# The second block of w1's columns in two parts: one load of six chunks becomes loads of two and of four

## The chip, the cores and the metric

The kernel runs on one core of a Trainium2 chip. The metric is device time in microseconds (us) of one execution. Matrix products run on TensorE (PE; its weight loads are listed as PEld), elementwise work on VectorE (DVE) and ScalarE (ACT), a few masks on GpSimd (POOL); SyncE (SP) issues most of the DMA transfers, ScalarE a few.

## What is computed

Two blocks share one layer norm of a sequence of 2048 tokens of width 448, and the second gates the first:

```python
xn = _layernorm(x)                       # (1, 2048, 448)
# A: linear attention, 16 heads of 28
q, k, v = split(xn @ wqkv)               # wqkv 448 x 1344
phi = lambda t: jnp.where(t > 0, t + 1, jnp.exp(t)) + 1e-6
kv = einsum("bhsd,bhse->bhde", phi(k), v); z = phi(k).sum(over s)
s = (phi(q) @ kv / (phi(q) . z + 1e-6)) @ wo
# B: a dense block with a squared relu
h = xn @ w1 + b1                         # w1 448 x 1792
g = silu(relu(h)**2 @ w2 + b2)           # w2 1792 x 448
out = x + s * g
```

All arrays are bfloat16.

## The kernel before

**Tiles.** Tokens stand in 16 tiles of 128 and four groups of four tiles (512 tokens). The width of 448 is contracted in three chunks of 128 rows (the "main" part of a weight) and one of 64. Those last 64 rows are loaded twice, into partitions 0 to 63 and 64 to 127 (the two "rests" of a weight), so that two half-height matmuls can run side by side in the two halves of TensorE. The 1792 columns of w1 are 14 chunks of 128; the product of group g with chunk fi is called H*g*.*fi*. K*si* is the key product of token tile si, Q*g*.*m* a query product, G*si* the gate product with w2.

**The order of work.** Every step is added to a list as an operation with its engine, what it reads and writes, and an estimated duration (`Program.add`). `Program.schedule` (L76 to L246) plays this through once: TensorE and SyncE keep the written order, and ScalarE, VectorE and GpSimd take their steps by readiness and due time. The planner also hands out the eight PSUM banks, in the order in which it expects them free. A DMA with an entry in the table `landing` (L1272) is taken to land at that time. What comes out is one fixed list for every engine and a set of semaphore waits (`Program.emit`). On the chip an engine does its list strictly in order.

**The start.** SyncE issues the loads in the written order (L453 to L469): x tiles 0, 1 and 2 to 3; the key weights; w1's first block (chunks 0 to 3) with its two rests; b1; w1's second block (chunks 4 to 9) with its two rests; x tiles 4 to 7; w1's third block (chunks 10 to 13) with its two rests. Then `late_loads` adds the row of b2, the two halves of w2 and the query weights with their rests, and after these follow x tiles 8 to 11 and 12 to 15, the value weights and wo. All of SyncE's transfers go through one queue that feeds the core's 16 DMA engines.

`load_main` (L435) is one DMA of 384 rows (three chunks of 128), `load_rest` (L442) with `part` one DMA of 64 rows. A row of the transfer is as long as the block is wide, two bytes for each column. `cuts` (L451) holds the blocks' borders, and `hh` (L781) makes a product wait for the main part and both rests of the block that its chunk lies in (names "w10", "w11", "w12").

**TensorE's first microseconds.** TensorE warms up on dummies (L1221), transposes x tiles 0 to 3 (L602, L626), and works on K0, K1, H0.0 and H0.1 as their data come (L801, L816, L829, L845). From there on the written order is H0.2 to H0.13 (L1360): `pe_four` takes four chunks at a time as two pairs that alternate, in the order H0.2 with H0.3 (first part, 8 matmuls), H0.4 with H0.5 (8), H0.2 with H0.3 (rest, 6), H0.4 with H0.5 (6), then likewise H0.6 with H0.7 and H0.8 with H0.9, then H0.10 with H0.11 and H0.12 with H0.13. All of these matmuls stand at L786. After them come K2, K3, G0 to G3 (L729, L1092), and Q0.0, Q0.1 (L739).

**VectorE beside it.** A K product becomes its feature map in three steps: the exponential on ScalarE (L707), a minimum (L712) and a maximum (L719) on VectorE. The last of them reads the product's PSUM bank for the last time. By the planner, VectorE's list around 11 us is: the maximum of K0, the layer-norm statistics of tiles 4 and 5 (L495 twice, L496 twice; they read x tiles 4 to 7's load), then the minimum and the maximum of K1, then the normalisation of tiles 4 and 5 (L525). H0.8 and H0.9 take the banks of H0.1 and K1.

Of the kernel before, what the change touches and what calls it, by code (L numbers as in the profile page):

```python
# [9 lines left out]
P = 128  # L10
S, D, F = 2048, 448, 1792
# [35 lines left out]
class Program:  # L47
# [6 lines left out]
    def add(self, eng, emit, reads=(), writes=(), dur=0.2, alts=(), nbytes=0, mode=None, label="", slow=1.0):  # L54
        op = Op(eng, emit, reads, writes, dur, alts, nbytes, mode, label)
        op.slow, op.behind, op.at = slow, None, None
        for t in op.reads:
            op.raw.add(self.writer[t])
            self.readers.setdefault(t, []).append(op)
        for t in op.writes:  # L60
            w = self.writer.get(t)
            if w is not None and w is not op:
                op.deps.add(w)
            for r in self.readers.get(t, ()):
                if r is not op:
                    op.deps.add(r)
            self.writer[t] = op
            self.readers[t] = [r for r in self.readers.get(t, ()) if r is op]
        op.raw.discard(op)
        op.deps |= op.raw  # L70
        for d in op.deps:
            d.succ.append(op)
        self.ops.append(op)
        return op
# [233 lines left out]
def bass_recurrent_scan__linear_attn_block__dense_activation_squared_relu__prompt_kernel(  # L308
    nc, A_x, A_wqkv, A_wo, B_x, B_w1, B_b1, B_w2, B_b2, out
):  # L310
    with ExitStack() as es:
# [21 lines left out]
        w_1 = sb("w_1", [P, 4, F], bf)  # L333
        w_2 = sb("w_2", [P, NF, D], bf)
        w_o = sb("w_o", [P, 7, D], bf)
        b1r = sb("b1r", [NF, P], bf)
# [83 lines left out]
        def tiles(t, lo, hi):  # L420
            if hi <= 2:
                return t[0][P * lo : P * hi].rearrange("(p s) d -> p s d", s=1)
            base, n = (2, 2) if hi <= 4 else (lo // 4 * 4, 4)
            v = t[0][P * base : P * (base + n)].rearrange("(p s) d -> p s d", s=n)
            return v[:, lo - base : hi - base, :]

        def dma(eng, dst, src, writes, nbytes, reads=(), dur=0.45, slow=1.0):
            return add(
                eng, lambda e, _: e.dma_start(dst, src), reads, writes, dur, nbytes=nbytes, label="dma" + str(writes[0]), slow=slow
            )  # L430

        def load_x(lo, hi, eng="sp"):
            dma(eng, x_tok[:, lo:hi, :], tiles(A_x, lo, hi), [("x", i) for i in range(lo, hi)], (hi - lo) * P * D * 2)

        def load_main(eng, w, src, name, lo, hi, c0=0, c1=3, off=0):  # L435
            dma(
                eng, w[:, c0:c1, lo:hi],
                src[128 * c0 : 128 * c1, off + lo : off + hi].rearrange("(c p) j -> p c j", p=P),
                [(name, c) for c in range(c0, c1)], 128 * (c1 - c0) * (hi - lo) * 2,
            )  # L440

        def load_rest(eng, w, src, name, lo, hi, off=0, part=None):  # L442
            for i in (0, 1) if part is None else (part,):
                dma(
                    eng, w[64 * i : 64 * i + 64, 3, lo:hi], src[384:448, off + lo : off + hi], [(name, 3 + i)],
                    64 * (hi - lo) * 2, ["actw"] if eng == "act" else (), dur=0.58,
                )

        wn = lambda name: [(name, i) for i in range(5)]
        HA = 2  # L450
        cuts = (0, 4 * P, 10 * P, F)  # L451
        add("act", lambda e, _: e.preload_act_table_set("natural_log_exp_and_others"), [], ["actw"], 1.25, label="table").prio = -1e6
        load_x(0, 1, "sp")  # L453
        load_x(1, 2, "sp")
# [5 lines left out]
        load_rest("sp", w_1, B_w1, "w10", cuts[0], cuts[1], part=0)  # L460
        load_rest("sp", w_1, B_w1, "w10", cuts[0], cuts[1], part=1)
        dma("sp", b1r[:, :], B_b1.rearrange("(f p) -> f p", p=P), ["b1r"], F * 2)
        load_main("sp", w_1, B_w1, "w11", cuts[1], cuts[2])
        load_rest("sp", w_1, B_w1, "w11", cuts[1], cuts[2], part=0)
        load_rest("sp", w_1, B_w1, "w11", cuts[1], cuts[2], part=1)
        load_x(4, 8, "sp")
        load_main("sp", w_1, B_w1, "w12", cuts[2], cuts[3])
        load_rest("sp", w_1, B_w1, "w12", cuts[2], cuts[3], part=0)
        load_rest("sp", w_1, B_w1, "w12", cuts[2], cuts[3], part=1)  # L469
        late_constants()  # L470

        def late_loads():
# [789 lines left out]
        for first, order in (  # L1262
# [6 lines left out]
                byname[b].prio = first + 1 + i  # L1269
            if first < -26:  # L1270
                byname[names[0]].prio = first
        landing = {("x", 0): 2.92, ("x", 1): 3.9, ("x", 2): 4.65, ("wk", 0): 5.7, ("wk", 3): 5.7, ("wk", 4): 7.2, ("w10", 0): 6.97, ("w10", 3): 7.2, ("w10", 4): 7.4, ("b1r", None): 7.5, ("w11", 0): 9.1, ("w11", 3): 9.4, ("w11", 4): 9.8, ("x", 4): 11.3}  # L1272
        for (name, k), t in landing.items():
            byname["dma" + str((name, k) if k is not None else name)].at = t

# [134 lines left out]
```

## Time and profile before

| | |
|---|---|
| median of 3 runs | 143.88 us (143.44 to 144.38) |
| the profiled execution's own time | 143.17 us |
| its span, first to last instruction | 141.9 us |
| TensorE busy | 138.5 us, 98% |
| VectorE, ScalarE, GpSimd busy | 103.0, 79.1, 6.2 us |
| DMA | 12.91 MB, mean 91 GB/s over the span |
| DMA engines' busy share | 0.9 or more from 3.5 to 17.7 us |

Times in the profile count from the first instruction. A row of the timeline gives start, length, engine, line, operation, output tile <- input tiles, the number of instructions merged, and in brackets the idle time before it and what ended it. In the DMA lists a row is tile <- source, issuing queue, count, KB each, and the us from issue to landing; in this trace all tiles of w1 and w2 are called `w`, K's `pk`, PSUM banks `pb`. A row of the table by stretches gives the stretch, its length, each engine's busy time, TensorE's granted clock, the share of the DMA engines that was busy (a little over 1 when packets overlap) and GB/s.

### The profile page before, as it was taken

What the parts mean: (1) busy time and instruction counts of PE and PEld (TensorE: products, weight loads), DVE (VectorE), ACT (ScalarE), POOL (GpSimd) and SP (SyncE); (2) the same over time, 40 slices, a digit from 0 to 9 for tenths busy, and PEclk for the clock granted to TensorE, in tenths of its full rate; (3) what the DMA queues carried; (4) which work ended last, traced back from release to release, by engine and by line L of the source; (5) the groups of instructions that cost most, each with busy time, mean ns of one, the idle gap of its engine ahead of it and who ended that gap; (6) DMA issues with size and microseconds to landing.
All of it is one profiled execution on the core that took longest, in us unless ns stands there. A gap on an engine that the chain in (4) does not pass through costs nothing.

```text
span 141.9 us, 3234 instructions
## 1 busy us (share of the span) xinstructions
PE 138.5 (98%) x1299; PEld 70.8 (50%) x1299; DVE 103.0 (73%) x222; ACT 79.1 (56%) x146; POOL 6.2 (4%) x40
## 2 busy tenths in 40 slices
PE   7999999999999999999999999999999999999992
PEld 7754445454444544444444444445547455555472
DVE  2756999699689897789777799786035516874875
ACT  3687998140888627697962767697139530301412
POOL 7900000000000000000000000000000000000000
PEclk9999999999999999999999999999999999999999
DMA  4999994239933000332000000000698000223033
GB/s 84 323 303 303 353 275 84 38 48 270 211 48 51 14 0 0 46 51 46 9 5 0 0 0 5 0 0 19 170 194 157 6 0 25 94 80 102 32 97 97
DMA packets 23516, 12.91 MB, mean 91 GB/s; under 512 B 14290, under 2 KB 22734, under 8 KB 23502
## 3 DMA queue, kind: packets, MB, share of 16 engines
q1 hardware_dynamic: 21710, 11.35, 31.5%
q10 hardware_dynamic: 1792, 1.36, 4.4%
q8 instruction: 10, 0.16, 0.5%
q14 instruction: 4, 0.03, 0.1%
HBM read 9.23 MB, written 1.90 MB: 78 GB/s over the span
## 4 chain that ended last, share of the span: by engine, by line
PE 97%; DVE 1%; issue 0%
PE pb L786 29%; PE pb L1092 22%; PE pb L1184 7%; PE pb L887 7%; PE pb L729 7%; PE pb L739 6%; PE pb L1109 4%; PE pb L1221 3%; PE pb L1149 3%; PE pb L866 1%; PE pb L829 1%; DVE gbuf L1173 1%; PE pb L893 1%; PE pb L801 1%; PE pb L1036 1%; PE pb L602 1%
## 5 line engine op out<-in xcount | busy, mean ns | idle before, releaser
L786 PE MATMUL pb<-xT,w 64*128 64x512 bf16 x378 | 43.6, 376 | 0.0
L1092 PE MATMUL pb<-w,r 64*128 64x448 bf16 x336 | 34.6, 349 | 0.0
L764 ACT ACTIVATE r<-pb,b1f 128x512 bf16<-128x512 f32 x40 | 25.7, 685 | 14.4 <-PE pb L786 14.1
L786 PEld LDWEIGHTS pb<-xT,w 64*128 64x128 bf16 x378 | 18.2, 94 | 21.9 <-DVE pk L719 0.3
L1092 PEld LDWEIGHTS pb<-w,r 64*128 64x128 bf16 x336 | 16.2, 94 | 16.0 <-issue 0.4
L776 ACT ACTIVATE r<-r 128x1024 bf16<-128x1024 bf16 x15 | 15.7, 1062 | 0.3
L761 DVE TENSOR_SCALAR r<-pb,b1f 128x512 bf16<-128x512 f32 x16 | 11.7, 744 | 4.1 <-PE pb L786 4.0
L1204 DVE TENSOR_TENSOR gbuf<-pb,gbuf 128x448 bf16<-128x448 f32 x14 | 8.1, 617 | 6.7 <-PE pb L1184 6.7
L495 DVE BATCH_NORM_STATS2 st<-x_tok 128x6 f32<-128x448 bf16 x16 | 9.6, 615 | 3.5 <-DMA x_tok<-in_A_x_dram 3.4
L729 PE MATMUL pb<-w_k,xT 64*128 64x448 bf16 x98 | 11.5, 349 | 0.0
L739 PE MATMUL pb<-xT,w_q 64*128 64x512 bf16 x84 | 11.0, 376 | 0.0
L1132 ACT ACTIVATE gbuf<-gbuf 128x448 bf16<-128x448 bf16 x14 | 7.0, 570 | 7.0 <-DVE gbuf L1082 5.9
L1184 PE MATMUL pb<-w_k,pqT 64*128 64x448 bf16 x96 | 10.5, 349 | 0.0
L1082 DVE TENSOR_TENSOR gbuf<-pb,b2b 128x448 bf16<-128x448 f32 x14 | 8.0, 613 | 3.4 <-PE pb L1092 2.0
L1000 DVE TENSOR_TENSOR pqT<-pqT,xT 128x2048 bf16<-128x2048 bf16 x3 | 3.7, 1222 | 8.5 <-DMA xT<-scr 8.5
L719 DVE SCALAR_TENSOR_TENSOR pk<-pb,pk 128x448 bf16<-128x448 f32 x16 | 9.6, 619 | 0.2
L707 ACT ACTIVATE pk<-pb 128x448 bf16<-128x448 f32 x16 | 7.8, 543 | 3.2 <-PE pb L729 2.5
L887 PE MATMUL pb<-pk,xn 128*128 128x448 bf16 x48 | 9.6, 353 | 0.0
L707 ACT ACTIVATE pqT<-pb 128x512 bf16<-128x512 f32 x12 | 6.5, 597 | 4.4 <-PE pb L739 4.4
L775 DVE TENSOR_TENSOR r<-r 128x1024 bf16<-128x1024 bf16 x13 | 8.6, 685 | 0.1
L923 DVE TENSOR_TENSOR zacc<-zacc,pk 128x448 f32<-128x448 f32 x13 | 8.0, 617 | 0.1
L525 DVE TENSOR_SCALAR xn<-x_tok,mv,rstd 128x448 bf16<-128x448 bf16 x16 | 7.4, 496 | 0.6 <-ACT rstd L507 0.6
(100 smaller groups left out, 133.4 us busy)
## 6 DMA issues: line engine op xcount, KB each, us to landing
w<-in_B_w_dram SPq DMA_DIRECT2D x2, 784.0 KB, 9.2
out_dram<-gbuf SPq DMA_DIRECT2D x14, 112.0 KB, 1.7
x_tok<-in_A_x_dram SPq DMA_DIRECT2D x3, 448.0 KB, 5.5
xT<-gbuf SPq DMA_DIRECT2D x32, 32.0 KB, 2.0
w<-in_B_w_dram SPq DMA_DIRECT2D x2, 384.0 KB, 5.7
xT<-scr SPq DMA_DIRECT2D x6, 112.0 KB
w<-in_B_w_dram SPq DMA_DIRECT2D x1, 576.0 KB, 5.4
xT<-scr ACTq DMA_DIRECT2D x5, 112.0 KB
```

The costliest lines, as they stand in the source:

```text
L495: add("dve", lambda e, _: e.bn_stats(st6[:, si, :], x_tok[:, si, :]), [("x", si)], [("st", si)], 0.61, label=f"bn{si}").prio = hp(si, 0)
L707: "act", lambda e, _: e.activation(out=slot, in_=ps(buf)[0:rows, 0:n], func=AF.Exp), [buf, "actw"],
L719: lambda e, _: e.scalar_tensor_tensor(out=slot, in0=ps(buf)[0:rows, 0:n], scalar=1.0 + 1e-6, in1=slot, op0=ALU.add, op1=ALU.max),
L729: return e.matmul(ps(b)[:, 0:D], x_tile(rows, si, c), w_k[rows, c, :], start=start, stop=stop)
L739: return e.matmul(ps(b)[:, 0:512], w_q[rows, c, m * P : (m + 1) * P], x_group(rows, g, c), start=start, stop=stop,)
L761: return e.tensor_scalar(out=slot, in0=ps(b)[:, 0:512], scalar1=b1f[:, fi : fi + 1], scalar2=0.0, op0=ALU.add, op1=ALU.max)
L764: return e.activation(out=slot, in_=ps(b)[:, 0:512], func=AF.Relu, bias=b1f[:, fi : fi + 1])
L776: return e.activation(out=both, in_=both, func=AF.Square)
L786: return e.matmul(ps(b)[:, 0:512], w_1[rows, c, fi * P : (fi + 1) * P], x_group(rows, g, c), start=start, stop=stop,)
L887: last = e.matmul(ps(b)[:, 0:D], xn_cols(si, c * P, (c + 1) * P), pk[:, si, :], start=(si == 0), stop=(si == NT - 1),)
L1092: return e.matmul(ps(b)[:, 0:D], r_cols(rows, fi, si), w_2[rows, fi, :], start=start, stop=stop)
L1184: return e.matmul(ps(b)[:, 0:D], w, msb[rows, c, :], start=start, stop=stop)
```

## The change

The second block of w1's columns is cut in two: chunks 4 and 5, and chunks 6 to 9. Each part has its own main DMA and its own two rests, so that three DMAs (576 KB, 96 KB, 96 KB) become six (192, 32, 32 and 384, 64, 64 KB), issued in this order ahead of x tiles 4 to 7. The last block is now called "w13". H0.4 and H0.5 (and the same chunks of the later groups) read "w11", H0.6 to H0.9 read "w12". The table `landing` has entries for the two parts in place of the one; the entry of x tiles 4 to 7 stays 11.3. The lists of TensorE, ScalarE, VectorE and GpSimd are in the order of before; SyncE's has three more issues.

```diff
-        cuts = (0, 4 * P, 10 * P, F)
+        cuts = (0, 4 * P, 6 * P, 10 * P, F)
...
-        load_main("sp", w_1, B_w1, "w11", cuts[1], cuts[2])
-        load_rest("sp", w_1, B_w1, "w11", cuts[1], cuts[2], part=0)
-        load_rest("sp", w_1, B_w1, "w11", cuts[1], cuts[2], part=1)
-        load_x(4, 8, "sp")
-        load_main("sp", w_1, B_w1, "w12", cuts[2], cuts[3])
-        load_rest("sp", w_1, B_w1, "w12", cuts[2], cuts[3], part=0)
-        load_rest("sp", w_1, B_w1, "w12", cuts[2], cuts[3], part=1)
+        for i in (1, 2, 3):
+            name = f"w1{i}"
+            load_main("sp", w_1, B_w1, name, cuts[i], cuts[i + 1])
+            load_rest("sp", w_1, B_w1, name, cuts[i], cuts[i + 1], part=0)
+            load_rest("sp", w_1, B_w1, name, cuts[i], cuts[i + 1], part=1)
+            if i == 2:
+                load_x(4, 8, "sp")
...
-        landing = {..., ("w11", 0): 9.1, ("w11", 3): 9.4, ("w11", 4): 9.8, ("x", 4): 11.3}
+        landing = {
...
+            ("w10", 3): 7.2, ("w10", 4): 7.4, ("b1r", None): 7.5, ("w11", 0): 8.2, ("w11", 3): 8.4, ("w11", 4): 8.6,
+            ("w12", 0): 9.7, ("w12", 3): 9.9, ("w12", 4): 10.1, ("x", 4): 11.3,
+        }
```

More of the change, by code (lines that the diff above doesn't have):

```diff
@@ L1271, in bass_recurrent_scan__linear_attn_block__dense_activation_squared_relu__prompt_kernel @@
                 byname[names[0]].prio = first
-        landing = {("x", 0): 2.92, ("x", 1): 3.9, ("x", 2): 4.65, ("wk", 0): 5.7, ("wk", 3): 5.7, ("wk", 4): 7.2, ("w10", 0): 6.97, ("w10", 3): 7.2, ("w10", 4): 7.4, ("b1r", None): 7.5, ("w11", 0): 9.1, ("w11", 3): 9.4, ("w11", 4): 9.8, ("x", 4): 11.3}
+        landing = {
[3 rows of a table added]
+        }
         for (name, k), t in landing.items():
```

1 row of the table landing is left out of this document.

## The prediction

> **What bounds the kernel now.** I read the chain that ended last first, because the change touches only loads of the first 20 us.
>
> ```profile
> PE 97%; DVE 1%; issue 0%
> ...
> 10.51 0.32 PE pb L845 x2
> 10.83 9.06 PE pb L786 x84
> ```
>
> TensorE sets the end nearly everywhere. From 10.83 us it works through the first group's H products (twelve column chunks, two of head work before them): 84 matmuls in 9.06 us, 0.108 us each, or 0.216 us for the two half-height matmuls of one step. The later run of 92 takes 9.93 us, the same 0.108. So this stage holds no gap that a faster load could close, in this execution. But two of its steps have nothing to spare. The timeline of weight loads shows them; the first row is the first weight load of H0.4 and H0.5, the ninth of this line (10.45 + 4 x 0.216 = 11.31).
>
> ```profile
> 11.32 0.53 PEld L786 LDWEIGHTS pb<-xT,w 64*128 64x128 bf16 x6
> ...
> 10.45 3.77 PEld L786 LDWEIGHTS pb<-xT,w 64*128 64x128 bf16 x36
> 14.53 0.56 PEld L786 LDWEIGHTS pb<-xT,w 64*128 64x128 bf16 x8 [0.30 <-DVE pk L719]
> ```
>
> The 37th weight load (after 8 + 8 + 6 + 6 + 8 = 36) is the first of H0.8 and H0.9. It was due at 10.45 + 18 x 0.216 = 14.34, came at 14.53, and waited for a VectorE instruction. A weight load runs one step (0.216) ahead of its matmul, so 0.19 of late start used up all but 0.03 us of that lead. What VectorE did before it:
>
> ```profile
> 10.57 0.62 DVE L719 SCALAR_TENSOR_TENSOR pk<-pb,pk 128x448 bf16<-128x448 f32 x1
> 12.28 1.15 DVE L495 BATCH_NORM_STATS2 st<-x_tok 128x6 f32<-128x448 bf16 x2 [1.09 <-DMA x_tok<-in_A_x_dram]
> 13.35 0.30 DVE L496 BATCH_NORM_AGGREGATE mv<-st 128x2 f32<-128x6 f32 x2
> 13.57 0.25 DVE L712 TENSOR_SCALAR pk<-pk 128x448 bf16<-128x448 bf16 x1
> 13.85 0.62 DVE L719 SCALAR_TENSOR_TENSOR pk<-pb,pk 128x448 bf16<-128x448 f32 x1
> ```
>
> The order is fixed: the statistics of token tiles 4 and 5 stand ahead of the last two steps on K1. VectorE idles 1.09 us for x tiles 4 to 7, and only then, at 14.47, releases the PSUM bank of K1 that the 37th weight load takes. **Thus the landing of x tiles 4 to 7 is on TensorE's path with 0.03 us to spare**. How that load stands in the DMA queue (SyncE's issues, then time from issue to landing):
>
> ```profile
> 5.14 1.58 SPq L429 DMA_DIRECT2D w<-in_B_w_dram  x3
> 6.76 0.59 SPq L429 DMA_DIRECT2D x_tok<-in_A_x_dram  x1
> 7.38 1.63 SPq L429 DMA_DIRECT2D w<-in_B_w_dram  x3
> ...
> w<-in_B_w_dram SPq DMA_DIRECT2D x1, 576.0 KB, 5.4
> ...
> w<-in_B_w_dram SPq DMA_DIRECT2D x1, 96.0 KB, 5.2
> ...
> x_tok<-in_A_x_dram SPq DMA_DIRECT2D x1, 448.0 KB, 5.5
> ```
>
> The second block's main part lands at 5.14 + 5.4 = 10.5, its last rest at 6.11 + 5.2 = 11.3, x at 6.76 + 5.5 = 12.3. The DMA engines are full in that time:
>
> ```profile
> 9.00:10.00 1.00, 0.96 (x10) 0.56 (x9) 0.36 (x1) 0.80 (x4) 0.00 (x0) 1.00 1.11 292
> 10.00:11.00 1.00, 1.00 (x11) 0.51 (x11) 0.71 (x2) 0.78 (x3) 0.00 (x0) 1.00 0.98 305
> 11.00:12.00 1.00, 1.00 (x14) 0.42 (x10) 0.19 (x1) 1.00 (x2) 0.00 (x0) 1.00 1.03 359
> ```
>
> The last two columns are their share, about 1, and GB/s. x waits for bytes ahead of it, not for its issue.
>
> **The change, part by part.**
>
> *What it removes.* Chunks 4 and 5 no longer wait for chunks 6 to 9. Their 256 KB (192 and twice 32) follow the first block, whose last rest lands at 8.3 (issued 3.84, 4.5 to landing), and at the 290 KB/us of now (384 KB of the third block land 1.32 us after x) they are there near 9.3 instead of 11.3. The weight load at 11.32 then has 2 us of margin. Its present wait lasts about 0: worth 0 here. In executions with later transfers it is worth what the load is late, but the bank of K1 follows 3.2 us later and takes the gain back if x is as late. I count 0, with 0.7 us as the bound, the median's distance from the profiled execution.
>
> *Three more DMAs on SyncE.* The present three take 6.76 - 5.14 = 1.62 us of issue, so x is issued at 8.38, the last block from 9.0, b2b at 10.7, w2 at 11.3 and 11.8, wq at 12.4. That is covered by the full engines: x's bytes begin when the rests ahead of it are in, near 11.0 (it lands 1.0 after the last rest), and a lone DMA needs 2.1 us from issue to landing (the first x tile, 112 KB). 8.38 + 2.1 plus the further 336 KB at 290 (1.2) gives 11.7, ahead of 12.3: 0.6 us of cover. Gone, x would come up to 1.62 late. For wq the cover is greater still: its issue alone now takes 2.98 us on a full queue.
>
> *Shorter rows.* The same 768 KB come as rows of 512 and 1024 bytes instead of 1536. No load here has 512-byte rows. Below: 0, since rows of 1024 (384 KB in 1.32 us, 291 KB/us) and of 896 (w2's second half, 784 KB 2.8 us after the first, 280) move no slower than those of 1536 (576 KB 2.2 us after the first block's last rest, 262). Above: the rows of 128 bytes at 23 to 24 us, 98 GB/s at a share of 0.64, so 153 GB/s when full; 256 KB at that rate instead of 290 cost 0.8 us. A cost per row explains both ends: with 1/153 and 1/290 us per KB at 128 and 1024 bytes, 512 bytes give about 1/257, which is 0.12 us for 256 KB, and the step from 1536 to 1024 another 0.08 for 512 KB. **I take 0.2 us**; 512 is nearer to 896 than to 128. Less than nothing is excluded: nothing ahead of x shrinks.
>
> *More completions in the queue.* The third block's second rest (64 KB) lands 0.15 us after its first (8.41 + 5.7 against 7.86 + 6.1), less than its bytes need at 290. I see no fixed price: 0, at most 3 x 0.2 = 0.6 if each new DMA held the queue like such a rest. [...]
>
> *The waits on TensorE.* H0.6 and H0.7 now wait for the new middle part. Everything on TensorE is queued behind them, but they start with the 29th weight load, 13.47, and the part is in by 11.3 + 0.2 = 11.5: 0. A passed wait costs nothing visible; the three for the last block (needed at 16.5, landed at 14.1) stand within the even 0.216 steps.
>
> *Loads behind.* w2 lands at 17.8 and 20.6, used at 20.3 and 23.6; wq's last rest at 22.0, used at 24.84; with 0.2 us all keep 2 us or more. x tiles 8 to 11 land at 22.9 and VectorE takes them at 22.98: no cover there, but TensorE and VectorE are by then late by the same 0.2. The planner keeps 11.3 for x, so K1's work stays behind the statistics.
>
> *The sum.* x 0.2 later, bank of K1 0.2 later, 0.03 of lead: TensorE loses 0.2 us at 14.5 and, being busy 97% of the chain, never finds it again. The profiled execution took 143.17 (span 141.9, 1.3 around it) and would take 143.4. The median shown is 143.88, 0.71 above; I add the same 0.2 to it: **144.1**.
>
> **The rivals.**
>
> *x bound by its issue (slower).* If more than now lies between an issue and its first bytes, x lands 5.5 us after 8.38, at 13.9, and the bank of K1 costs TensorE 1.6: 145.5, +1.1%. It decides from 0.6 us of lost cover on. For it: all three mechanisms needed are seen, a fixed VectorE order, no slack, 1.62 us of issue. Against: the DMA share of 1 until x has landed.
>
> *A price for each DMA.* 3 x 0.2 = 0.6: 144.5. Against it the 0.15 us between two rests. [...]
>
> *The wait for the second block was the real one.* In executions above the profiled one, TensorE may stand at 11.32 for a late rest while x is in time. Then the change gives back up to 0.7: 143.2 to 143.6. For it: the wait ends at exactly the moment of need, and the median is 0.71 longer. Against: x lies behind the same bytes.
>
> *It doesn't do what it says.* The planner could lay banks otherwise with new landing times; more than 1% faster would need this or something else that I don't see, since no more than 0.5 us of TensorE's time here waits for w1 at all (for the first block, not touched).
>
> **How the numbers follow.** Forecast 0.62, price for each DMA 0.06, the second block's wait 0.12, issue 0.14, more than 1% faster 0.04, other losses 0.02. Range 143.3 to 145.5: it takes in the gain of the third case, the upper bound of the rows (0.8) and the issue case; the likeliest case's own is 143.7 to 144.7. A measurement of this kernel tells about 1% from no change. Faster by over 1%: 0.04; within: 0.80; slower: 0.16.
>
> **What would show it.** In the changed profile the weight load near 11.32 follows a landing 1.5 us or more earlier; VectorE's statistics start at 12.3 to 12.9; the 37th weight load comes as much after 14.53 as x is late, and the run of 84 lasts 9.06 plus this. Wrong: the statistics at 13.5 or later (issue), or the run of 84 unchanged with x late (slack that I missed), or a loss away from this stage.

## The result and the profile after

The changed kernel took 144.82 us in the median of 22 runs (143.73 to 147.52), the kernel before, run beside it, 143.61 (142.98 to 144.38). The ratio is 1.0069 with a 95% interval of 1.0047 to 1.0090: the change costs 0.7%, about 1.0 us. The ratios here leave out executions more than 1.5% above the fastest of the same kernel, of the changed kernel here two of 22 (147.10 and 147.52 us, with a mean granted clock of 0.988 in place of 1.0).

The profiled execution took 145.70 us, its span 144.4, so 2.5 more than the profiled one of before. It is one of the longer ones; that the shorter ones have in small what it shows in large is likely, but none of them was profiled. The chain that ended last now leaves TensorE ahead of 17 us: first its shares, then its first three long pieces (start, length, what).

```profile
PE 86%; SPq 5%; DMA 4%; DVE 3%; issue 1%
...
8.55 6.22 DMA x_tok<-in_A_x_dram
14.79 1.15 DVE st L495 x2
17.04 5.36 PE pb L786 x48
```

The 5% of SPq are SyncE's issues up to 8.55, among them the six of the second block: the chain goes back through the queue of loads. The load of x tiles 4 to 7 (called x below) takes 6.22 us from its issue (5.5 before), VectorE's statistics wait for it, and TensorE waits for VectorE. VectorE's timeline:

```profile
10.91 0.62 DVE L719 SCALAR_TENSOR_TENSOR pk<-pb,pk 128x448 bf16<-128x448 f32 x1
14.79 1.15 DVE L495 BATCH_NORM_STATS2 st<-x_tok 128x6 f32<-128x448 bf16 x2 [3.26 <-DMA x_tok<-in_A_x_dram]
15.87 0.30 DVE L496 BATCH_NORM_AGGREGATE mv<-st 128x2 f32<-128x6 f32 x2
16.08 0.24 DVE L712 TENSOR_SCALAR pk<-pk 128x448 bf16<-128x448 bf16 x1
16.36 0.62 DVE L719 SCALAR_TENSOR_TENSOR pk<-pb,pk 128x448 bf16<-128x448 f32 x1
```

It idles 3.26 us in place of 1.09. The weight loads show where this arrives:

```profile
10.80 3.77 PEld L786 LDWEIGHTS pb<-xT,w 64*128 64x128 bf16 x36
17.04 0.98 PEld L786 LDWEIGHTS pb<-xT,w 64*128 64x128 bf16 x12 [2.47 <-DVE pk L719]
```

The same 36 weight loads run evenly, and the 37th, that of H0.8, comes at 17.04 in place of 14.53: 2.51 later, as much as x (in at 14.77, before at 12.26), and that is the whole difference of the spans. What is new is in the DMA columns (the last two of the table by stretches: share of the DMA engines, GB/s). The two stretches from 10 to 11 us, of the changed kernel:

```profile
10.00:10.50 0.50, 0.47 (x5) 0.43 (x6) 0.00 (x0) 0.50 (x3) 0.00 (x0) 1.00 0.52 88
10.50:11.00 0.50, 0.50 (x6) 0.19 (x5) 0.36 (x2) 0.50 (x2) 0.00 (x0) 1.00 0.63 143
```

and of the kernel before:

```profile
10.00:10.50 0.50, 0.50 (x7) 0.27 (x7) 0.25 (x1) 0.50 (x2) 0.00 (x0) 1.00 1.00 298
10.50:11.00 0.50, 0.50 (x7) 0.24 (x8) 0.47 (x2) 0.28 (x2) 0.00 (x0) 1.00 0.96 312
```

The engines run half empty just when x should be moving. (Part of the lost bytes is lost earlier: from 8 to 9 us, behind the first part's rests, the engines moved 213 GB/s against 369 before. But e2 and e11 below have the same early dip, 227 and 232, and lose no time.) SyncE's queue shows what they lack:

```profile
5.13 3.38 SPq L429 DMA_DIRECT2D w<-in_B_w_dram  x6
8.55 0.58 SPq L429 DMA_DIRECT2D x_tok<-in_A_x_dram  x1
```

Six issues take 3.4 us for 768 KB, 225 KB/us, less than the 292 to 369 GB/s that the engines moved in the kernel before from 8 to 11 us. By the completion counts of the load, fifteen of the sixteen engines had x in at 13.04 us (12.13 before), and the last one at 14.77 (12.26).

### The profile page after: what moved, and what is told of

Its sections match the earlier page's. It is cut to its first block, busy times and chain, and to the rows that moved or that the text cites. A ratio compares the mean times of both kernels' runs of the same rounds, so it can differ in the third digit from the quotient of the medians.

```text
span 144.4 us, 3238 instructions
## 1 busy us (share of the span) xinstructions
PE 138.2 (96%) x1299; PEld 71.0 (49%) x1299; DVE 103.1 (71%) x222; ACT 79.1 (55%) x146; POOL 6.8 (5%) x40
## 3 DMA queue, kind: packets, MB, share of 16 engines
q1 hardware_dynamic: 22270, 11.35, 31.4%
## 4 chain that ended last, share of the span: by engine, by line
PE 86%; SPq 5%; DMA 4%; DVE 3%; issue 1%
PE pb L786 26%; PE pb L1092 22%; PE pb L1184 7%; PE pb L887 6%; PE pb L729 6%; PE pb L739 6%; SPq L429 5%; DMA x_tok<-in_A_x_dram 4%; PE pb L1109 4%; PE pb L1149 3%; PE pb L866 1%; DVE gbuf L1173 1%; PE pb L893 1%; PE pb L1036 1%; DVE st L495 1%; PE pb L961 1%
```

## The experiments

Two theories stood at the start: ISSUE, that x comes too late into the queue because of three more issues, and ROWS, that rows of 512 and 1024 bytes hold the engines longer than rows of 1536. "Before" in the runs below is the kernel before, run beside each of them. In every kernel here the lists of TensorE, ScalarE and GpSimd are those of before, VectorE's too but for the swap where that is the experiment.

| run | loads ahead of x | x issued | a tenth of x's packets begun | 15 engines / all landed | ratio to before (95%) |
|---|---|---|---|---|---|
| before | 3 | 6.76 | 9.74 | 12.13 / 12.26 | 1 |
| changed | 6 | 8.55 | 10.99 | 13.04 / 14.77 | 1.0069 (1.0047 to 1.0090) |
| e10, changed again | 6 | 8.56 | 11.02 | 12.86 / 14.88 | 1.0053 (1.0028 to 1.0077) |
| e1, three tiny loads | 3 + 3 | 8.16 | 9.59 | 12.46 / 13.30 | 1.0003 (0.9980 to 1.0026) |
| e9, four tiny loads | 3 + 4 | 8.61 | 9.83 | 12.13 / 12.33 | 1.0006 (0.9987 to 1.0025) |
| e7, 512 rows of 32 bytes | 3 + 1 | 7.38 | 9.65 | 13.07 / 13.92 | 1.0020 (0.9989 to 1.0051) |
| e5, short rows, 3 issues | 3 | 6.54 | 9.52 | 12.11 / 12.67 | 0.9966 (0.9947 to 0.9985) |
| e6, rests joined | 4 | 7.36 | 10.29 | 12.34 / 12.47 | 0.9977 (0.9955 to 0.9999) |
| e11, x ahead of two rests | 4 | 7.33 | 9.62 | 11.87 / 12.01 | 0.9989 (0.9972 to 1.0006) |
| e2, x ahead of the middle part | 3 | 6.75 | 8.47 | 10.56 / 11.26 | 0.9976 (0.9957 to 0.9995) |
| e8, e2 with K1 first | 3 | 6.75 | 8.24 | 10.27 / 10.41 | 0.9971 (0.9950 to 0.9993) |

Columns three to five (us) are from one profiled execution each, read from the trace's packets of 3584 bytes (one row of x tiles 4 to 7) and the load's completion counts; the ratio is from all timed runs.

**e1: only the issues.** The kernel before with three small DMAs ahead of x.

```diff
+        [dma("sp", spare[:, k, :], B_b1.rearrange("(f p) -> f p", p=P), [("spare", k)], F * 2) for k in range(3)]
         load_x(4, 8, "sp")
```

> The kernel before with three small DMAs (3.5 KB each, b1 into a spare tile that nothing reads) issued between the second block's last rest and x tiles 4 to 7. Same rows and bytes of w1 in three loads, no new wait on TensorE; only SyncE's issue of x moves, from 6.76 to about 8.6 us. Theory ISSUE (the three extra issues bring x behind the point where the DMA engines run dry): x lands 0.7 us or more later than 12.26, the engines' share falls well under 1 between 10 and 11 us as in the changed kernel, and the time is 0.4 to 0.9% above the kernel before. Theory ROWS (the rows of 512 and 1024 bytes hold the engines longer, the issue is covered): x lands at 12.3 to 12.4 and the time is within 0.2% of the kernel before.

x was issued at 8.16, not at 8.6: these small loads took less of SyncE than counted. The engines stayed full (shares of 1.04 from 10 to 10.5 and again to 11), and the median did not move. The profiled execution was a long one (144.22 us): fifteen engines had x in at 12.46, the last at 13.30, and TensorE's weight loads stood still for 0.96 us ahead of H0.8. ISSUE, as it was stated, missed: 1.4 us later in the queue costs nothing in the median while the bytes ahead are there early.

**e9: a fourth small load**, to match the changed kernel's issue time.

> As the run with three small DMAs ahead of x tiles 4 to 7, with four of them, so that x is issued at about 8.6 us, where the changed kernel issues it, while the 768 KB ahead of it are issued by 6.7 as before. If the late issue of x is by itself what costs, x lands 0.7 us or more later than in the kernel before and the time is 0.4 to 0.9% above it. If the bytes issued early keep the engines busy until x comes (they are busy to 11.3), the engines' share stays near 1 from 10 to 11 us, x lands by 12.6 but for a single late engine, and the time is within 0.25% of the kernel before.

SyncE's timeline of this run:

```profile
5.10 1.56 SPq L429 DMA_DIRECT2D w<-in_B_w_dram  x3
6.70 1.86 SPq L429 DMA_DIRECT2D spare<-in_B_b_dram  x4
8.61 0.37 SPq L429 DMA_DIRECT2D x_tok<-in_A_x_dram  x1
```

x is issued at 8.61, later than in the changed kernel, and is in by 12.33. The time is within 0.25% of before. There was a dip of the share to 0.50 from 10 to 10.5 us, against the expectation, so half-empty engines by themselves are not the loss either. But a tenth of x's packets had begun 1.2 us after its issue, ahead of that dip; in the changed kernel it took 2.4 us. So the late issue alone is not the cause.

**e2: x ahead of the middle part**, otherwise the changed kernel.

```diff
-            if i == 2:
+            if i == 1:
                 load_x(4, 8, "sp")
```

> The changed kernel with x tiles 4 to 7 issued between the two parts of the second block, so after the first part's rests (issue near 6.75 us as before, with 512 KB fewer bytes ahead of it). ISSUE and ROWS both have x early: landing near 10.7 to 11.0, VectorE's statistics begin at once after the maximum of K0 (11.2 to 11.5), the bank of K1 comes by 13.4 and the late weight load of H0.8 is gone. The middle part lands near 12.5 to 13.0, against 13.5 where it is needed. If the bank of K1 is all that the change costs, the time is that of the kernel before or up to 0.4% lower (executions with a late x gain). If the two parts cost something of their own (more DMAs, more waits), it stays above the kernel before.

The statistics start at 11.35 without a wait, the run of 84 matmuls has no gap, and the time is 0.24% below the kernel before. The same loads with the same rows and waits, in another order, cost nothing. So the loss hangs on x's place in the queue.

**e5: short rows without more issues.** Both main loads, but one load of 128 rows for all rests.

```diff
             load_main("sp", w_1, B_w1, name, cuts[i], cuts[i + 1])
+            if i == 1:
+                dma("sp", w_1[:, 3, cuts[1] : cuts[3]], B_w1[320:448, cuts[1] : cuts[3]], [("w11", 3), ("w11", 4)], P * 768 * 2)
```

> Two main loads (chunks 4 and 5 with rows of 512 bytes, chunks 6 to 9 with rows of 1024) but one load of 128 rows of 1536 bytes in place of all rests: three issues as in the kernel before, x issued near 6.75, 896 rows ahead of x after the first block against 512 before and 1024 in the changed kernel. It leaves part of the computation out: the lower copy of the last 64 rows is filled with the 64 rows ahead of them. Theory FEED (x's first packets wait for the number of rows to be handed out ahead of them, at about 3 ns a row as the 512 rows of the run with x first suggest, 6.5 to 8.0 us): x's first packet near 9.3 to 10, x lands 12.3 to 13, 0.2 to 0.6% above the kernel before. Theory SMALL LOADS (the four loads of 64 rows and their issues are what starves the engines): x as in the kernel before or earlier, time within 0.2%.

FEED was a version of ROWS that I formed after e2, and it missed: x's packets begin as before (9.52 against 9.74), fifteen engines have x in as before (12.11 against 12.13), and with rows of 512 and 1024 bytes the time is 0.34% lower.

**e6: one more issue.** The rests of chunks 4 to 9 stay in two loads.

```diff
+            if i != 2:
+                load_rest(..., cuts[i], cuts[i + 1 if i > 1 else 3], part=0); load_rest(..., part=1)
+            else:
                 load_x(4, 8, "sp")
```

> The changed kernel with the rests of chunks 4 to 9 left in two loads (rows of 1536 bytes) behind the first main part: four issues in place of six, x issued near 7.2, 896 rows ahead of it. FEED: x lands nearly as late as in the changed kernel (12.6 to 13), time 0.3 to 0.6% above the kernel before. SMALL LOADS: x near 12.3 to 12.5, time within 0.2% of the kernel before.

x lands at 12.47, as SMALL LOADS had it, and the time is 0.23% below before rather than equal. Its mains are the changed kernel's, rows and all; only the rests differ. **Two 64-row loads fewer ahead of x, and with them an issue of x 1.2 us earlier, make the difference between -0.2 and +0.7%.** The two stretches from 10 to 11 us:

```profile
10.00:10.50 0.50, 0.50 (x6) 0.39 (x4) 0.04 (x1) 0.50 (x2) 0.00 (x0) 1.00 1.10 360
10.50:11.00 0.50, 0.50 (x6) 0.21 (x6) 0.47 (x2) 0.36 (x1) 0.00 (x0) 1.00 1.04 393
```

**e7: many rows, few bytes.** One load of 512 rows of 32 bytes ahead of x.

```diff
+        dma("sp", spare[:, :, 0:16], ap(B_w1, [[F, P], [448, 4], [1, 16]]), [("spare", 0)], P * 128)
         load_x(4, 8, "sp")
```

> The kernel before with one more load between the second block and x: 512 rows of 32 bytes (16 KB) into a spare tile that nothing reads; one more issue (about 0.5 us), almost no bytes. FEED: these 512 rows delay x as the changed kernel's do: x's first packets come after 9.8, the engines fall below a share of 0.8 for some half microsecond near 10 to 11.5, x lands 12.7 or later, time 0.2 to 0.6% above the kernel before. If instead the engines' own time per byte is what the short rows cost, 32 rows for each engine at some 10 ns are 0.3 us: x lands near 12.5, time within 0.25%.

Unclear in time (+0.2%, the interval from -0.1 to +0.5). x's packets began at 9.65, so FEED is wrong here too, but x landed late (13.92), and so did the second block: H0.4's weight load waited 0.96 us for it. From 9 to 10 us the engines were at a share of 1.31 for 217 GB/s (before 1.11 for 292), so the rows of 32 bytes seem to slow them; this says nothing of rows of 512. The 10 ns a row of the expectation are an estimate; the nearest that a trace shows are the packets of 128 bytes in the kernel before, 12 ns in the median from 22 to 25 us.

**e11 and e10: only the last two rests, and the changed kernel again.** e11 issues x after the main load of chunks 6 to 9 and ahead of its two rests.

```diff
             load_main("sp", w_1, B_w1, name, cuts[i], cuts[i + 1])
+            if i == 2:
+                load_x(4, 8, "sp")
             load_rest("sp", w_1, B_w1, name, cuts[i], cuts[i + 1], part=0)
             load_rest("sp", w_1, B_w1, name, cuts[i], cuts[i + 1], part=1)
-            if i == 2:
-                load_x(4, 8, "sp")
```

> The changed kernel with x tiles 4 to 7 issued after the main load of chunks 6 to 9 and ahead of its two rests: the same nine loads of w1 and x, the same rows, x issued near 7.4 in place of 8.55. If the two small loads just ahead of x are what lets the engines run dry, they stay full to 11.5 us, x lands by 12.4, the two rests land near 12.7 against 13.5 where they are needed, and the time is that of the kernel before or up to 0.3% below it. If six loads in place of three cost by themselves, 0.3% or more above it remain.

> The changed kernel, unaltered, beside the other runs of this call. The 0.7% should return (0.4 to 1.0%), and the profile should again show the DMA engines at a share under 0.8 in a stretch between 10 and 11 us, x's load of tiles 4 to 7 ending at 13.0 or later, and a gap of TensorE before H0.8. If engines are full there and the time still is 0.7% above, the starving is not the cause.

With two loads of 64 KB moved behind x the loss is gone (0.9989; the changed kernel, run beside it, had 1.0053). This moves x's issue 1.2 us forward too; that a late issue is harmless without the rests is what e9 adds. From 10 to 11 us, e11:

```profile
10.00:10.50 0.50, 0.46 (x5) 0.42 (x6) 0.00 (x0) 0.50 (x3) 0.00 (x0) 1.00 0.99 394
10.50:11.00 0.50, 0.50 (x6) 0.20 (x5) 0.35 (x2) 0.50 (x2) 0.00 (x0) 1.00 1.01 343
```

and e10:

```profile
10.00:10.50 0.50, 0.50 (x7) 0.27 (x6) 0.28 (x1) 0.50 (x2) 0.00 (x0) 1.00 0.71 94
10.50:11.00 0.50, 0.50 (x6) 0.20 (x4) 0.49 (x1) 0.28 (x2) 0.00 (x0) 1.00 0.42 86
```

The starving is repeated in e10 and absent in e11. The two rests ahead of x, issued some 0.6 us apart, bring 64 KB each to engines that moved about 150 KB in 0.5 us in the kernel before.

**e3 and e12: K1 first, with the changed loads.** The swap in VectorE's list, made after the planning:

```diff
+        d = pr.order["dve"]
+        d.remove(mi); d.remove(ma)          # minimum and maximum of K1
+        d[d.index(bn) : d.index(bn)] = [mi, ma]   # ahead of tile 4's statistics
```

> The changed kernel with one swap in VectorE's list, made after the planning: minimum and maximum of K1 ahead of the statistics of tiles 4 and 5; all other lists and the loads as in the changed kernel. If x's landing costs through the bank of K1, the bank comes at about 12 us instead of 14.5 to 17, and the 2 us gap at the 37th weight load is gone. x is still late, so that the normalisation and with it the relu of H0.5 on VectorE come later; the bank of H0.5 is needed at 17.4, so a late x (13 to 14.8) costs 0 to 0.7 us there. Time: 0.2 to 0.8% below the changed kernel, near the kernel before. If the cost lies elsewhere, it stays at +0.7%.

> One more look at the changed kernel with K1 first in VectorE's list, whose times went from 143.0 to 145.4. If this profile is one above 144.5, its loss should lie after H0.8: in a late relu of H0.5 on VectorE, whose bank H0.12 takes, or in a late transfer of the second half of w2 or the query weights. If it is near 143, it shows again no gap in the run of 84 matmuls though x is late.

The median of e3's twelve executions is 144.12 us, 0.36% above the kernel before (143.61), where the changed kernel's is 0.84% above: the swap takes away a little over half. Their times go from 142.98 to 145.39; without the three longest, 145.22 and above, the ratio is 1.0005 (0.9970 to 1.0040). Its profile (143.50) has x in at 13.22 and all 84 weight loads in one even run of 8.95 us. e12 (145.32) shows why the spread stays. Its x came at 15.20:

```profile
15.99 0.74 PEld L786 LDWEIGHTS pb<-xT,w 64*128 64x128 bf16 x8
18.41 2.73 PEld L786 LDWEIGHTS pb<-xT,w 64*128 64x128 bf16 x28 [1.67 <-ACT r L764]
```

The 37th weight load, that of H0.8, no longer waits, though x is later than in the changed kernel's profile (15.20 against 14.77): that confirms the path through the bank of K1. The gap has moved 20 weight loads on, to H0.10, and two waits end there 0.07 us apart. One is ScalarE's: the layer norm of tiles 4 and 5 stands ahead of the relus in its list and waited 3.04 us for the statistics, so the relu that frees the next bank ended only at 18.31. The other is w1's third block: its last rest was in at 14.80 on fifteen engines and at 18.35 on one, and TensorE's queue waited for it until 18.38. Either alone would have held TensorE to nearly the same moment. I had expected the relu on VectorE; it was ScalarE's, and beside it a load that I had not named. ScalarE's row, and that of the first matmuls after the gap:

```profile
16.63 0.29 ACT L503 ACTIVATE vep<-mv,eps 128x2 f32<-128x2 f32 x1 [3.04 <-DVE mv L496]
18.44 3.20 PE L786 MATMUL pb<-xT,w 64*128 64x512 bf16 x28 [1.20 <-DMA w<-in_B_w_dram]
```

**e4 and e8: the swap in the kernel before, and with x first.**

> The kernel before with the same swap in VectorE's list. Its profiled execution had 0.03 us to spare at this place, others are up to 1.2 us longer. If these lose their time by a late x through the bank of K1, the swap takes it away: 0.2 to 0.5% below the kernel before and a narrower spread. If not, within 0.1%.

> x tiles 4 to 7 ahead of the middle part and, in VectorE's list, K1 ahead of the statistics. With x early neither order waits, so the bank of K1 comes at about 12.1 in place of 13.5, both ahead of need: the time is that of the run with x first, 0.2 to 0.3% below the kernel before, and no better than this by more than 0.1%.

e4: 0.9980 (0.9961 to 0.9999), times from 143.08 to 143.87. So the kernel before seems to lose a little to a late x as well; the interval only just leaves out 1. e8: 0.9971 (0.9950 to 0.9993), with a profile in which nothing in this stage waits for x; it is below both kernels, by 0.3 and about 1%. Against e2 (0.9976) the swap adds nothing that can be told.

## Why the prediction was right, and where a size was off

**The path was right.** The load of x tiles 4 to 7, VectorE's fixed order, the bank of K1, the 37th weight load with 0.03 us to spare: the changed profile shows each. e2 and e11 take the loss away by an earlier x; e3 frees the bank of K1 from x and takes a little over half away, since a late x then holds up ScalarE's relus. The first part did come earlier, its last rest at 9.71 us (forecast 9.3; the whole block before 11.27), and in the two profiled executions no wait of TensorE was there for it to remove, as forecast. Slower, and by less than 1%, was right too, and the range held.

**The size was not.** Forecast +0.2 us, measured +1.0 (2.5 in the profiled execution). The measured 144.82 lies just outside the 143.7 to 144.7 of the forecast's own case, and the statistics at 14.79 are what the prediction itself had named as a sign of being wrong (13.5 or later: the issue). The step that failed is "three more DMAs on SyncE", put at nothing with 0.6 us of cover. The cover was worked out with the latency of a lone load (2.1 us to landing, some 1.0 to its first packets: the first x tile was issued at 0.81 and its packets began at 1.84) and with engines that are full until x comes. Both failed in the changed kernel: a tenth of x's packets had begun only 2.4 us after the issue, and the engines ran at a share of 0.52 to 0.63 from 10 to 11 us. Fifteen engines had x 0.9 us later than before, and the sixteenth 1.7 us after that. Nor did x's bytes begin near 11.0 in the kernel before: their first packet is at 9.26, and a tenth had begun by 9.74.

**Shorter rows**, the 0.2 us that I took, cost nothing that the runs show (e5, e6). So the forecast was nearer to the truth than its reasons, and that it was near is partly luck: the term that I counted is absent, and the one that I set to nothing is all that is seen.

**x bound by its issue**, the rival with 0.14, named the right mechanism and the point from which it decides (lost cover); its price of 1.6 lies between the 1.0 of the comparison and the 2.5 of the profile. Its 5.5 us from issue to landing were 4.5 for fifteen engines and 6.2 for the last. It is half right: e1 and e9 show that the same late issue is harmless where the bytes ahead were issued early. It takes the small loads directly ahead of x as well.

**A price for each DMA**: no. Three and four tiny loads cost +0.03 and +0.06% (both intervals take in 0), so no run shows the 0.2 us for each new DMA that this rival counted. e2 and e11 have the changed kernel's six loads in the same sizes without a loss, so the loads lose by their place, not by their number.

**The second block's wait as the real one**: partly. In e7 and e9 H0.4's weight load did wait for the second block (0.96 and 0.47 us), and e6, with the early first part and x no earlier than before, is 0.2% faster. The earlier first part is probably worth a little where x's place is kept. I had given this 0.12; by this reading the change brought the gain and lost more.

**Waits on TensorE and loads behind** cost nothing in the changed kernel's profile, as said: outside the gap the weight loads run evenly. In e12 a load behind x did come too late (the third block's last rest, 18.35).

## What to carry to other kernels

In this kernel a full DMA queue covered late issues only while what was issued kept it full (x issued at 8.61 us in e9 and at 8.55 in the changed kernel, ratios 1.0006 and 1.0069). Reckon bytes per issue against what the engines move: 64 KB for 0.6 us of SyncE is about a third of the 305 GB/s that the engines moved in the kernel before from 10 to 11 us, so put such loads behind the one that somebody waits for. An engine that waits in a fixed list held up what stood behind it (here the release of a PSUM bank: K1's minimum ran at 13.57 us behind the statistics in the kernel before, at 11.42 ahead of them in e4); look for the load behind such a wait before shifting any load ahead of it.

## What the runs showed of the hardware

- **The time from an issue to its packets is not fixed.** For the same load of x, issued at 8.5 to 8.6 us, a tenth of its packets had begun 1.2 us later behind four loads of 14 rows, and 2.4 to 2.6 us later behind 64-row rests (changed, e3, e10, e12), where the engines' share fell to between 0.35 and 0.75 from 10 to 11 us. What in the rests makes it longer was not settled.
- **One late engine.** In three of the four profiles with these loads one of the sixteen engines delivered x 1.7 to 2.2 us after the fifteenth (14.77, 14.88, 15.20); in e3 it did not. Its executions are the longer ones (145.70, 147.46 and 145.32 us against 143.50), so it is likely to make the spread of the changed kernel. In the changed kernel's profile the share of all engines fell to 0.21 from 14 to 14.5 us, while the last one still worked on x. Its cause is open.
- **A gap in this stage may cost twice.** This is one execution. In e10's profiled execution the weight loads paused for 2.98 us, and then TensorE's granted clock (the third column from the right) fell to half:

```profile
17.00:18.00 1.00, 0.85 (x6) 0.31 (x8) 1.00 (x4) 1.00 (x3) 0.00 (x0) 0.56 1.08 368
18.00:19.00 1.00, 1.00 (x8) 0.44 (x6) 1.00 (x3) 0.57 (x1) 0.00 (x0) 0.50 1.09 358
19.00:20.00 1.00, 1.00 (x8) 0.31 (x4) 1.00 (x3) 0.00 (x0) 0.00 (x0) 0.50 1.11 338
20.00:21.00 1.00, 1.00 (x10) 0.38 (x8) 1.00 (x4) 0.65 (x2) 0.00 (x0) 0.74 1.14 314
```

That execution took 147.46 us. Its pause was 2.98 us for the weight loads and 2.49 for the matmuls; after the pause in the changed kernel's profile, 2.47 and 2.0 us, the clock stayed at 1.00. What brought the fall in the one and not in the other was not shown.
